# Chunk attention and two gated products on one core: opening, loads around the bursts, banks and sums in another order

## The chip, the cores and the metric

The kernel runs on one core of a Trainium2 chip. The metric is the device time of one execution in microseconds (us), the median of several runs; the profile and the trace are of one further execution.

## What is computed

The reference, cut to what matters (q, k and v are 8 x 8 x 576 x 64, float32):

```python
q_c, k_c, v_c = (t.reshape(8, 8, 9, 64, 64) for t in (q, k, v))   # chunks of 64
scores = scale * q_c @ k_c.transpose(0, 1, 2, 4, 3)
attn = softmax(scores)                                            # per row, 1e-9 in the divisor
x = (attn @ v_c) -> tokens x 512                                  # 4608 x 512
x = (x @ w_a) * (x @ w_b) @ w_out                                 # inner width 1536
out = ((x @ w1) * (x @ w2)) @ w3 @ w_out2                         # inner width 1024
```

## The kernel before

**Tiles and stages.** The 4608 tokens are 9 blocks of 512. The first gated product goes through its inner width in 12 slices f of 128, the second in 8. All large products are kept accurate by splitting each operand into a high part and a low part (fp32r) and doing three TensorE (PE) products for each one wanted. For a block and a slice, the first products x·w_a and x·w_b are `pa` and `pb` (L901), their gated product is split into `gh` and `gl` (L287 on ScalarE, L288), and the second product with `wo` is summed over f in four PSUM banks (`acc`, L944).

- *Opening.* Attention of block 0 is done unit by unit (a unit is one pair of heads of one block; `U[0]` to `U[3]`): load q and k (`load1`), load v (`load2`), `turn` (transposes `t`, copies `qT`, `kT`), `scores` (`s`), `soft1` (maximum `mx`, exponent `e`), `soft2` (sum `sm`, its reciprocal, a multiplication of `e`), `flip` (`f`, `pT`), `apply` (`x`), `put`. Beside it the weights w_a, w_b and w_out are converted into their two parts by jobs of the class Pump: three VectorE (DVE) operations L209, L212 and L220 with a ScalarE one between, then a ScalarE cast and a low part (L725 on VectorE for w_a and w_b, on GpSimd for w_out). `pump.load` issues a job's load, `begun` its first part, `run` its second part and the low part of the job before, `flush` the low part alone.
- *Plain steps.* Blocks 0 and 1, slice by slice, with `pa` and `pb` (`plain_step`). The first slices of block 0 come while weights are converted.
- *Burst.* The gated products of a pair's second block are kept, and its second products are done all in a row: 12 slices of 12 `acc` products (`burst`). Such a slice needs its `wo`, 512 KB, loaded into one of four places.
- *Pass over a pair.* Blocks 2 and 3, 4 and 5, 6 and 7 go as pairs by Strassen's scheme: seven products P1 to P7 (L914) per slice on three banks, whose sums ScalarE copies (L1001) and VectorE adds (L1005); VectorE's L1034 makes the gated product (`strassen_step`). In the first pass VectorE also makes the sums of weights `su` that the scheme needs, and the attention of blocks 4 and 5. A burst stands between two passes.
- *Block 8 alone.* After the last burst come plain steps of block 8, and between them w3·w_out2 is made on the chip: parts of w3 are turned on PE (`w3p`, L1174) into `w3t`, and multiplied (`wf`, L1185), all on PSUM bank D. w_out2 and w3 come by small loads `o_0` to `o_7` and `w3_0` to `w3_15` (`load_small`, L1142) into four places; a part `o` is split into its two parts by `one` in `o2_pieces`, called from the burst.
- *Second gated product.* The same with w1, w2 and the fused weight.

**What sets the order.** Every engine works through its own instructions in the order of the code, and a DMA is issued by an engine's queue in the order of its instructions; a queue that waits holds all behind it. Nearly all loads are issued on SP's queue. The loads of attention units are put on a list (`ask`), and taken off it by `settle` (all that a unit needs) and by `tick(loads=n)`, which precedes each group of PE products; the number of `tick` in a `first` group is `state["pace"]`. VectorE work that can lie anywhere is cut into pieces, and a `Track` hands them out at the `point()` calls of a step; it keeps an estimate of how far PE and VectorE have come (class Engines) and holds a piece back where VectorE is ahead of that by `backlog`, or where a piece with PE work (`needs`) would come before `self.ready`.

## Time and profile before

| | |
|---|---|
| median of 3 runs | 1621.13 us (1620.41 to 1628.59) |
| profiled execution | 1621.47 us |
| its span in the trace | 1619.7 us |
| PE busy, idle | 1546.9 us, 72.8 us |
| opening, to the end of U[3] and the first slices | 0 to 113.2 us |
| plain steps | 113.2 to 262.2 us |
| first burst, first pass over a pair | 262.2 to 305.4, 305.4 to 478.3 us |
| second burst, second pass | 478.3 to 517.6, 517.6 to 675.1 us |
| third burst, third pass | 675.1 to 711.4, 711.4 to 864.8 us |
| last burst, block 8 with w3·w_out2 | 864.8 to 907.2, 907.2 to 1062 us |
| second gated product | 1062 to 1619.7 us |

The stages are cut where PE's first product of the next one starts. PE is the engine that is busy nearly always, so what can be read as lost is PE's idle time and the time in which its products run longer than elsewhere. In the trace's own times 1.8 us of the profiled execution lie outside the span.

### The profile page before, as it was taken

Reading aid. Unit: us, or ns where it says so; the run is one execution under the profiler, and the core shown is the slowest. Engines: PE = TensorE matmul, PEld = TensorE weight load, DVE = VectorE, ACT = ScalarE, POOL = GpSimd, SP = SyncE. Lnnn points to the kernel's source line nnn. Section 1 sums busy time; section 2 is a strip of 40 time slices with the busy share of each in tenths; the row PEclk is TensorE's granted clock in tenths of the full one; section 3 lists DMA queues with packets and bytes.
Section 4 is the critical chain, followed back from the end, with each engine's and each line's share of the span. In section 5 each row is a group of like instructions: output and inputs, shape, how many; then the busy total and the mean of one; then the engine's idle time right before and its main releaser. Section 6 shows DMA issues by size and latency. Waiting matters only on the chain.

```text
span 1619.7 us, 24157 instructions
## 1 busy us (share of the span) xinstructions
PE 1546.9 (96%) x8968; PEld 1254.5 (77%) x8968; DVE 856.1 (53%) x1384; ACT 539.9 (33%) x997; POOL 491.0 (30%) x502
## 2 busy tenths in 40 slices
PE   5689999998999999999999899999999999999998
PEld 4568787776777787888787777888878878878887
DVE  5767564776757555576775235545532442442431
ACT  4444444332334222433334223333421421421322
POOL 0323324322234211433235212223522422422422
PEclk9889999998999999999999999999999999999999
...
GB/s 245 216 240 266 255 152 187 262 218 225 241 100 216 200 226 218 130 211 342 334 292 171 286 318 325 300 275 256 115 226 221 74 223 222 74 217 209 68 289 155
DMA packets 277013, 356.31 MB, mean 220 GB/s; under 512 B 174240, under 2 KB 194720, under 8 KB 276896
## 3 DMA queue, kind: packets, MB, share of 16 engines
...
HBM read 268.70 MB, written 85.98 MB: 219 GB/s over the span
## 4 chain that ended last, share of the span: by engine, by line
PE 80%; DVE 7%; issue 4%; DMA 3%; ACT 3%; SPq 2%; POOL 1%; DVEq 0%; POOLq 0%; ACTq 0%
PE P L914 41%; PE acc L944 22%; PE pa L901 4%; PE pb L901 4%; PE wf L1185 3%; PE pa0L L901 2%; DMA wo<-dwo 1%; PE x L442 1%; SPq L181 1%; PE s L390 1%; PE pb0L L901 1%; DVE c L1005 1%; PE t L519 1%; DMA qk<-in_k_dram 1%; ACT xP L287 1%
## 5 line engine op out<-in xcount | busy, mean ns | idle before, releaser
L914 PE MATMUL P<-xP,w 128*128 128x512 f32 (+1 forms) x3066 | 698.3, 381 | 13.7 <-DVE c L1005 8.5
L914 PEld LDWEIGHTS P<-xP,w 128*128 128x128 f32 x3066 | 553.8, 189 | 129.8 <-DVE c L1005 12.6
L1005 DVE TENSOR_TENSOR c<-P,c 128x512 f32<-128x512 f32 (+1 forms) x228 | 150.5, 661 | 322.2 <-PE P L914 321.7
L1001 ACT COPY c<-P 128x512 f32<-128x512 f32 (+1 forms) x228 | 128.6, 564 | 226.4 <-PE P L914 226.1
L1036 POOL TENSOR_TENSOR G<-c,c 128x512 f32<-128x512 f32 x68 | 89.3, 1313 | 319.6 <-DVE c L1005 319.5
L287 ACT CAST gh<-c 128x512 fp32r<-128x512 f32 x68 | 42.2, 621 | 316.6 <-DVE c L1034 316.6
L288 POOL TENSOR_TENSOR gl<-c,gh 128x512 fp32r<-128x512 f32 x68 | 90.7, 1333 | 177.6 <-ACT gh L287 177.6
L944 PE MATMUL acc<-gh,wo 128*128 128x512 f32 x384 | 138.3, 397 | 0.0
L944 PE MATMUL acc<-wo,gh 128*128 128x512 f32 x320 | 111.0, 390 | 0.5 <-ACT gh L287 0.5
L1034 DVE TENSOR_TENSOR c<-P,c 128x512 f32<-128x512 f32 x68 | 46.9, 689 | 120.9 <-PE P L914 120.9
L901 PE MATMUL pa<-xq,w 128*128 128x512 f32 x276 | 76.5, 431 | 9.9 <-DVE w L725 9.9
L944 PEld LDWEIGHTS acc<-gh,wo 128*128 128x128 f32 x384 | 72.4, 188 | 15.5
L288 DVE TENSOR_TENSOR xP<-xP,xP 128x512 fp32r<-128x512 f32 (+1 forms) x56 | 65.4, 1209 | 22.9 <-ACT xP L287 22.9
L944 PE MATMUL acc<-gl,wo 128*128 128x512 f32 x192 | 75.0, 391 | 0.0
L901 PEld LDWEIGHTS pa<-xq,w 128*128 128x128 f32 x276 | 56.3, 209 | 23.7 <-DVE w L725 10.4
L944 PEld LDWEIGHTS acc<-wo,gh 128*128 128x128 f32 x320 | 60.1, 188 | 13.0 <-ACT gh L287 1.0
L901 PE MATMUL pb<-xq,w 128*128 128x512 f32 x276 | 68.5, 397 | 0.0
L954 ACT COPY ev<-acc 128x512 f32<-128x512 f32 x72 | 42.4, 588 | 72.9 <-PE acc L944 67.9
L944 PE MATMUL acc<-wo,gl 128*128 128x512 f32 x160 | 62.5, 390 | 0.8 <-POOL gl L288 0.8
L190 POOL DMA_DIRECT2D dw<-w x58 | 31.8, 551 | 89.8 <-DVE w L288 85.8
L901 PEld LDWEIGHTS pb<-xq,w 128*128 128x128 f32 x276 | 50.5, 188 | 10.4
L408 ACT ACTIVATE e<-e 128x512 f32<-128x512 f32 x36 | 22.8, 633 | 107.0 <-DVE e L402 103.2
...
## 6 DMA issues: line engine op xcount, KB each, us to landing
...
wo<-dwo SPq DMA_DIRECT2D x128, 512.0 KB, 4.5
...
```

What stands on the lines that cost most here:

```text
L190: queue.dma_start(to, src)
L287: nc.scalar.copy(dst_h, src)
L288: eng_l.tensor_tensor(dst_l, src, dst_h, op=ALU.subtract)
L901: nc.tensor.matmul(ps, w[m][:, kk // 2, wp, kk % 2], xq[kk // 2][:, kk % 2, xp], start=(begins and n == 0), stop=(ends and n == len(terms) ...
L914: nc.tensor.matmul(ps, w[:, wp, kt], x[:, kt, xp], start=(begins and n == 0), stop=(n == 5), skip_group_check=True,)
L944: nc.tensor.matmul(acc[m], a, b, start=(f == 0 and (wp, gp) == SEQ[0]), stop=(f == NF[ph] - 1 and (wp, gp) == SEQ[-1]),)
L954: nc.scalar.copy(t, acc[m])
L1001: nc.scalar.copy(t, src)
L1005: nc.vector.tensor_tensor(o, a, b, op=ALU.add)
L1034: nc.vector.tensor_tensor(g, last, c11, op=ALU.mult)
L1036: nc.gpsimd.tensor_tensor(g_place(ph, nm.split("_")[0], f, gplaces), c22, c12, op=ALU.mult)
L1185: nc.tensor.matmul(ps, t[:, gp, jj], wo2[jj // 2][:, jj % 2, wp], start=(jj == 0 and (wp, gp) == SEQ[0]), stop=(jj == NF[1] - 1 and (wp, g ...
```

## The change

It has five groups of edits.

1. *Opening.* q and k of U[3] are asked for earlier, v of U[0] and U[1] later (behind the transposes and the exponent of U[0]; both are issued on ScalarE's queue). Job 1 is begun after `soft2` of U[3] rather than amid the attention of U[0] to U[3]; jobs further on follow its low parts sooner, with `pump.ahead` 0 or 1 for a while; `flush` and `scores` move.
2. *Loads around bursts.* The pace of unit loads at the end of the plain steps goes from 5 to 9. What was spread over the first burst (sums of weights and weights, six loads) is issued ahead of it. Ahead of the last burst three conversion loads are issued at once; the first four w3 loads become pieces of it.
3. *Small loads.* `load_small` issues on ScalarE's queue instead of SP's (24 loads).
4. *Banks.* `w3p` and `wf` take turns on banks B and D.
5. *Order of sums and pieces.* In a Strassen step the sums with P3 and P7 follow each other, and the point for pieces comes after both. `Track` waits 0.9 us rather than 0.3 after a piece with PE work, and the backlog is 2.0 in two places (2.5, and none, before). Conversions in the first slices are handed out over 2 points rather than 5.

```diff
@@ -95,7 +95,7 @@
             if e and needs and cost < 1:
                 self.ready = e.pe + 1.5
             elif e and cost > 0.5:
-                done = e.computed(cost) + 0.3
+                done = e.computed(cost) + (0.9 if needs else 0.3)
                 if needs is not None:
...
@@ -1016,9 +1016,9 @@
         freed(1)
         point()
         add(c12, take("P3"), c12)
-        point()
         add(c22, take("P7"), c22)
         freed(2)
+        point()
         pend.part()
         pend.part()
         point()
...
     wo2, w3f, w3t = [], deque(), {}
-    small = {"n": 0}
+    small = {"n": 0, "bank": 0}
+
+    def either(name):
+        small["bank"] += 1
+        return bank("BD"[small["bank"] % 2], name)
 
     def load_small(src, name):
         small["n"] += 1
         t = pool.tile([P, NT], F32, tag=["qk0", "qk1", "ep0", "ep1"][small["n"] % 4], name=name)
-        nc.sync.dma_start(t, src)
+        nc.scalar.dma_start(t, src)
         return t
 
     def o2_pieces():
@@ -1169,7 +1173,7 @@
         w = w3f.popleft()
         if c == 0:
             w3t[i] = pool.tile([P, 2, NF[1], P], F32R, tag=f"G{i % 2}", name=f"w3t_{i}")
-        ps = bank("D", f"w3p_{i}_{c}")
+        ps = either(f"w3p_{i}_{c}")
         for m in range(4):
             nc.tensor.transpose(ps[:, m * P : (m + 1) * P], w[:, m * P : (m + 1) * P], ident)
         t = w3t[i]
@@ -1179,7 +1183,7 @@
 
     def fuse(i):
         t = w3t.pop(i)
...
@@ -1259,11 +1263,11 @@
                 load()
             settle(asks["all"])
 
-        asked(U[0].load1, U[1].load1, U[0].load2, U[1].load2)
+        asked(U[0].load1, U[1].load1)
         pump.load()
-        asked(U[2].load1)
+        asked(U[2].load1, U[3].load1, U[2].load2)
         pump.load()
-        asked(U[3].load1, U[2].load2, U[3].load2)
+        asked(U[3].load2)
         pump.load()
 
         plain = {0: {}, 1: {}}
@@ -1285,11 +1289,13 @@
             pump.begin(n)
 
         U[0].turn()
+        asked(U[0].load2)
         U[0].scores()
         pump.load()
         U[1].turn()
         U[0].soft1()
         begun(1)
+        asked(U[1].load2)
         U[1].scores()
         U[2].turn()
         U[0].soft2()
@@ -1297,7 +1303,6 @@
         U[1].soft1()
         pump.load()
         asked(U[4].load1)
-        begun(2)
         U[1].soft2()
         U[0].apply()
         U[0].put()
@@ -1307,7 +1312,6 @@
         U[2].soft1()
         pump.run()
         pump.load()
-        pump.run()
         U[1].apply()
         U[3].scores()
         U[3].soft1()
@@ -1315,6 +1319,9 @@
         U[1].put()
         U[2].flip()
         U[3].soft2()
+        pump.flush()
+        begun(2)
+        pump.run()
         pump.load()
         pump.load()
         pump.load()
@@ -1322,7 +1329,6 @@
         asked(U[5].load1)
         U[2].apply()
         U[2].put()
-        pump.flush()
         U[3].flip()
         xq = [quadrants[0, 0], quadrants[0, 1]]
         banks = [bank("AC"[m], f"p{m}0") for m in range(2)]
@@ -1333,7 +1339,8 @@
 
         features(0, [0, 1])
         U[3].apply()
-        pump.begin(pump.done + 1)
+        pump.flush()
+        begun(pump.done + 1)
         U[3].put()
         features(0, [2])
         U[4].turn()
@@ -1345,14 +1352,16 @@
         nc.scalar.copy(sa, banks[0])
...
         asked(U[4].load2)
+        U[4].scores()
         pump.run()
-        U[4].scores()
+        pump.ahead = 1
+        pump.run()
         U[4].soft1()
+        pump.flush()
         nc.vector.tensor_tensor(sa, banks[1], sa, op=ALU.mult)
         state["pending"] = Second(0, 0, 0, wouts[0], g_parts(sa, "0_0_0", nc.gpsimd), sums[0])
-        pump.run()
+        pump.ahead = 2
         pump.load()
-        pump.flush()
         U[5].load2()
         tick(loads=4)
         units = unit_list(1)
@@ -1363,7 +1372,8 @@
         at = None
         for n, (T, f) in list(enumerate(order))[1:]:
             if T == 0:
-                conv = Track([conv_piece()] * (4 if f == 1 else 3), 5 if f + 1 < AHEAD else 8, engines)
+                ahead = f + 1 < AHEAD
+                conv = Track([conv_piece()] * (4 if f == 1 else 3), 2 if ahead else 8, engines)
                 if f + 1 == NF[0]:
                     conv = None
             if T == 1 and f == 0:
@@ -1382,7 +1392,7 @@
             if n + 3 == len(order):
                 at.finish()
                 next_units(2)
-                state["pace"] = 5
+                state["pace"] = 9
             if n + 1 == len(order):
                 state["ready"] = ready(0, 1, NF[0] - 2, plain[0])
...
@@ -1423,7 +1433,7 @@
                     if k + 2 < n:
                         su[k + 2] = summed(ph, order[k + 2], k + 2)
                         su[k + 2].load()
-                    extra = Track(su[k + 1].pieces() if k + 1 < n else [], 5, engines)
+                    extra = Track(su[k + 1].pieces() if k + 1 < n else [], 5, engines, 2.0)
                 if whole_new:
                     if READY <= f + 2 < n:
                         su[f + 2] = Sums(ph, f + 2, dict(tag=f"Y{f % 2}"))
@@ -1528,20 +1538,17 @@
                 pieces = pieces + o2_pieces()
                 pump.cap = len(pump.jobs)
                 pump.homes(["xo1", "xo2"], ["G2"])
-                pieces += [(0.1, False, lambda: pump.load())] * 3
+                for _ in range(3):
+                    pump.load()
+                pieces += [(0.1, False, lambda n_=n_: load_w3(n_)) for n_ in range(4)]
             elif not begins:
                 x, pieces = strassen_pieces(x32, f"{ph}{sb}", sb == NSB)
             if ph == 0 and sb == 1:
-                begins_with = []
                 for n_ in range(2):
                     first_sums[n_] = summed(ph, orders[ph, sb][n_], n_)
-                    begins_with.append((0.1, False, first_sums[n_].load))
-                for n_, i in ((0, 0), (0, 3), (1, 0), (1, 3)):
-                    begins_with.append(
-                        (0.1, False, lambda f=orders[ph, sb][n_], i=i: load_part(ph, f, i))
-                    )
-                for n_, p in enumerate(begins_with):
-                    pieces.insert(4 + 3 * n_, p)
+                    first_sums[n_].load()
+                    for i in (0, 3):
+                        load_part(ph, orders[ph, sb][n_], i)
                 pieces = pieces + first_sums[0].pieces()
             steps, at, conv = NF[ph], [], []
             if ph == 0 and not lone:
@@ -1557,14 +1564,12 @@
                     conv = later_conv(3 * NF[1])
                     work = merged((0, 1, work), (0, 1, conv))
                     n_pts = PTS * steps
-                at.append(Track(work, n_pts - 1 if sb + 1 < NSB else n_pts - 3, engines, 2.5))
+                at.append(Track(work, n_pts - 1 if sb + 1 < NSB else n_pts - 3, engines, 2.0))
             if not begins:
                 done = (ph, sb - 1) if sb else (ph, 0)
                 burst(ph, j + 1, orders[done], places, pieces, [] if conv else at, state.pop("ready", None))
             if lone:
                 got = []
-                for n_ in range(4):
-                    load_w3(n_)
                 at.append(Track(between(got), 5 * steps - 15, engines))
                 xs = {}
 
```

Where it moves instructions, in three places.

**VectorE in the opening**, behind the sum `sa_0_1` of slice 1 (cv is a conversion, `sm` and `e` the softmax of unit U[4], w_2_0 the low part that slice 2's `pa` takes). Before:

```order
L1065 TENSOR_TENSOR sa_0_1_753<-pb_0_1_761,sa_0_1_753 128x512
L209 TENSOR_SCALAR cv_xo_556<-cv_xo_556 128x512
L212 SCALAR_TENSOR_TENSOR cv_xo_397<-cv_xo_556 128x512
L220 SCALAR_TENSOR_TENSOR cv_xo_397<-cv_xo_556,cv_xo_397 128x512
L413 TENSOR_REDUCE sm_0_808<-e_0_709 128x8
L414 TENSOR_SCALAR sm_0_808<-sm_0_808 128x8
L415 RECIPROCAL sm_0_808<-sm_0_808 128x8
L416 TENSOR_TENSOR e_0_709<-e_0_709,sm_0_808 128x512
L209 TENSOR_SCALAR cv_Y_266<-cv_Y_266 128x512
L212 SCALAR_TENSOR_TENSOR cv_Y_267<-cv_Y_266 128x512
L220 SCALAR_TENSOR_TENSOR cv_xo_397<-cv_xo_556,cv_xo_397 128x512
L725 TENSOR_TENSOR w_2_0_792<-cv_xo_397,w_2_0_792 128x2x256
```

After:

```order
L1065 TENSOR_TENSOR sa_0_1_750<-pb_0_1_769,sa_0_1_750 128x512
L209 TENSOR_SCALAR cv_Y_260<-cv_Y_260 128x512
L212 SCALAR_TENSOR_TENSOR cv_Y_261<-cv_Y_260 128x512
L220 SCALAR_TENSOR_TENSOR cv_xo_397<-cv_xo_557,cv_xo_397 128x512
L725 TENSOR_TENSOR w_2_0_766<-cv_xo_397,w_2_0_766 128x2x256
```

A conversion triple and the four softmax rows no longer stand ahead of the low part w_2_0; they stand behind w_3_0 now, or earlier.

**SP's queue around the first burst** (qk and v are loads of attention units, su and w those of the first pass, wo those of the burst). Before, from the burst's first load of a `wo` on:

```order
L181 DMA qk_1_2808<-in_q_dram 32x8x32 x4
L782 DMA wo_7_2991<-dwo_7_171 128x1024
L181 DMA qk_1_2808<-in_q_dram 32x8x32 x2
L819 DMA su_11_3005<-d_0_11_155 128x1024
L819 DMA su_10_3012<-d_0_10_154 128x1024
L181 DMA qk_1_2808<-in_q_dram 32x8x32 x2
L181 DMA qk_1_2808<-in_k_dram 32x8x32 x2
L797 DMA w_11_0_3039<-dw_11_0_108 128x1024
L181 DMA qk_1_2808<-in_k_dram 32x8x32 x2
L782 DMA wo_6_3054<-dwo_6_170 128x1024
L181 DMA qk_1_2808<-in_k_dram 32x8x32 x2
L799 DMA w_11_3_3068<-dw_11_1_109 128x512
```

After:

```order
L181 DMA v_1_2809<-in_v_dram 64x2x64 x4
L819 DMA su_11_2957<-d_0_11_155 128x1024
L797 DMA w_11_0_2959<-dw_11_0_108 128x1024
L799 DMA w_11_3_2961<-dw_11_1_109 128x512
L819 DMA su_10_2963<-d_0_10_154 128x1024
L797 DMA w_10_0_2965<-dw_10_0_104 128x1024
L799 DMA w_10_3_2967<-dw_10_1_105 128x512
L782 DMA wo_7_3025<-dwo_7_171 128x1024
L782 DMA wo_6_3074<-dwo_6_170 128x1024
L782 DMA wo_5_3101<-dwo_5_169 128x1024
L782 DMA wo_4_3126<-dwo_4_168 128x1024
```

The loads of the unit and the six for the pass stand ahead of wo_7 now, and the four `wo` loads follow each other.

**VectorE in the first pass**, slice 7 (the two L1005 rows are the sums with P3 and with P7; `sm`, `e` and `pT` are the softmax of a unit). Before:

```order
L1005 TENSOR_TENSOR c_7_3955<-P_7_3882,c_7_3955 128x512
L413 TENSOR_REDUCE sm_3_4000<-e_3_3979 128x8
L414 TENSOR_SCALAR sm_3_4000<-sm_3_4000 128x8
L415 RECIPROCAL sm_3_4000<-sm_3_4000 128x8
L416 TENSOR_TENSOR e_3_3979<-e_3_3979,sm_3_4000 128x512
L1005 TENSOR_TENSOR c_7_3889<-P_7_3918,c_7_3889 128x512
L422 STREAM_TRANSPOSE pT_3_4024<-e_3_3979 128x512
```

After:

```order
L1005 TENSOR_TENSOR c_7_3991<-P_7_3912,c_7_3991 128x512
L1005 TENSOR_TENSOR c_7_3922<-P_7_3953,c_7_3922 128x512
L413 TENSOR_REDUCE sm_3_4021<-e_3_3947 128x8
L414 TENSOR_SCALAR sm_3_4021<-sm_3_4021 128x8
L415 RECIPROCAL sm_3_4021<-sm_3_4021 128x8
L416 TENSOR_TENSOR e_3_3947<-e_3_3947,sm_3_4021 128x512
L422 STREAM_TRANSPOSE pT_3_4033<-e_3_3947 128x512
```

The sum with P7 stands right behind the sum with P3, and the four softmax rows behind both.

No engine has more or fewer instructions to compute with; ScalarE issues 24 DMAs more and SP 24 fewer.

## Rows read from the trace of the kernel before

**Rows 1.** The page, part 1: busy time, share of the span, instructions.
```profile
PE 1546.9 (96%) x8968; PEld 1254.5 (77%) x8968; DVE 856.1 (53%) x1384; ACT 539.9 (33%) x997; POOL 491.0 (30%) x502
```

**Rows 2.** Busy time by stage (windows): engines, granted clock, DMA share, GB/s.
```profile
0.00:113.20 113.20, 77.99 (x784) 61.19 (x784) 76.40 (x147) 51.38 (x99) 26.93 (x37) 0.86 0.83 232
262.19:305.42 43.23, 39.10 (x188) 30.68 (x189) 35.24 (x47) 19.34 (x35) 20.56 (x19) 0.96 0.84 246
305.42:478.28 172.86, 163.67 (x1115) 128.96 (x1114) 115.34 (x214) 49.91 (x95) 45.27 (x49) 0.97 0.69 209
517.56:675.06 157.50, 156.72 (x1114) 125.66 (x1114) 81.15 (x152) 38.48 (x72) 32.29 (x27) 1.00 0.74 204
675.06:711.40 36.34, 36.33 (x160) 29.77 (x160) 29.21 (x27) 18.55 (x33) 21.50 (x18) 1.00 0.49 162
864.84:907.19 42.35, 38.33 (x160) 30.62 (x159) 17.31 (x15) 17.31 (x31) 19.20 (x18) 0.96 0.59 204
```

**Rows 3.** TensorE's waits, 0 to 122 us: total us, times, longest us.
```profile
PE pa L901 <- DVE w L725: 9.9, 2, 5.5
PE t L519 <- DMA qk<-in_q_dram: 6.1, 1, 6.1
```

**Rows 4.** Timeline of ScalarE and its DMA queue, 0 to 10 us: start, us.
```profile
3.58 4.72 ACTq L181 DMA_DIRECT2D v<-in_v_dram  x4
8.33 1.28 ACT L520 ACT_TABLE_LOAD   x1 [8.33 <-DMA v<-in_v_dram]
```

**Rows 5.** Timeline of TensorE, 46 to 80 us, plain products.
```profile
46.49 5.25 PE L901 MATMUL pa<-xq,w 128*128 128x512 f32 x12 [5.45 <-DVE w L725]
51.58 2.88 PE L901 MATMUL pb<-xq,w 128*128 128x512 f32 x12
...
62.49 5.49 PE L901 MATMUL pa<-xq,w 128*128 128x512 f32 x12 [4.41 <-DVE w L725]
```

**Rows 6.** Timeline of VectorE, 54 to 63 us.
```profile
54.57 0.69 DVE L1065 TENSOR_TENSOR sa<-pb,sa 128x512 f32<-128x512 f32 x1 [5.70 <-PE pb L901]
...
57.97 0.67 DVE L413 TENSOR_REDUCE sm<-e 128x8 f32<-128x512 f32 x1
...
61.75 0.69 DVE L725 TENSOR_TENSOR w<-cv_xo,w 128x512 fp32r<-128x512 f32 x1
```

**Rows 7.** Line L220, 0 to 122 us: ns min/median/max.
```profile
L220 DVE SCALAR_TENSOR_TENSOR cv_xo<-cv_xo,cv_xo x8: 682/686/1796, 44.1 to 98.9; 128x512 int32<-128x512 int32 x8
```

**Rows 8.** TensorE's waits in the first burst, 262 to 306 us.
```profile
PE acc L944 <- DMA wo<-dwo: 4.1, 3, 2.5
```

**Rows 9.** Timeline of SP's DMA queue, 264 to 277 us.
```profile
265.27 0.36 SPq L782 DMA_DIRECT2D wo<-dwo  x1
...
275.93 0.34 SPq L782 DMA_DIRECT2D wo<-dwo  x1
```

**Rows 10.** TensorE's waits in the first pass over a pair, 306 to 478 us.
```profile
PE P L914 <- DVE c L1005: 5.4, 5, 1.8
PE P L914 <- DVE c L1034: 3.0, 1, 3.0
```

**Rows 11.** Busy time in part of that pass.
```profile
360.00:400.00 40.00, 35.13 (x219) 27.24 (x218) 26.29 (x50) 9.75 (x18) 7.60 (x8) 0.87 0.70 202
```

**Rows 12.** Timeline of VectorE, 385 to 394 us.
```profile
392.01 0.71 DVE L379 STREAM_TRANSPOSE kT<-qk 128x512 f32<-128x512 f32 x1 [3.74 <-DMA v<-in_v_dram]
```

**Rows 13.** TensorE's waits in the last burst, 860 to 905 us.
```profile
PE acc L944 <- DMA wo<-dwo: 4.0, 2, 2.3
```

**Rows 14.** Timeline of SP's DMA queue, 876 to 884 us.
```profile
880.47 2.02 SPq L1142 DMA_DIRECT2D o<-do  x2
882.55 0.42 SPq L782 DMA_DIRECT2D wo<-dwo  x1
```

**Rows 15.** TensorE's waits in the steps of block 8, 905 to 1060 us.
```profile
PE w3p L1174 <- DVE w3t L288: 3.5, 6, 1.7
PE wf L1185 <- DVE w3t L288: 1.3, 3, 0.7
```

2 lines of the change are left out of this document (1 added, 1 removed).

## Prediction

> **What bounds the kernel now.** I read the table of engines first. TensorE (PE) is busy for 1546.9 us of a span of 1619.7 [rows 1], so 72.8 us of idle time are all that a better order can win there, besides products that run slow. VectorE, at 53%, bounds no long stage; where it counts, it is late with one result.
>
> Then the stages, beside the same kind of stage without trouble [rows 2]. In the opening PE is busy for 77.99 of 113.20 us, at a granted clock of 0.86 of full speed. The first burst took 43.23 us, and the last 42.35; the third did the same products in 36.34, at 1.00. The first pass over a pair took 172.86 us and the second 157.50, where VectorE had 115.34 and 81.15 us to do. So the losses lie at the opening, two bursts and the first pass. These are where the change works, and in each I looked for what ended the waits.
>
> The profiled execution took 1621.47 us, 0.34 over the median of the runs; the sum is made against 1621.5, and the 1.8 us outside the span are taken as they are.
>
> **Opening.** PE waits 9.9 us in two places for VectorE's low part of a weight, and 6.1 for the first q and k [rows 3]. The two waits are ahead of the `pa` of slices 1 and 2. In the rows of PE, the `pa` behind them took 5.25 and 5.49 us, where the `pb` that followed took 2.88 for the same 12 products [rows 5]: the clock had fallen while PE waited. So each wait is paid about twice. On VectorE, the sum of slice 1 ended at 55.26 us, and the low part came at 61.75, after a conversion, four softmax rows from 57.97 on, and another conversion [rows 6]. The change takes the softmax and one of the two conversions out of this row, that is, the 3.78 us from 57.97 to 61.75, of a wait of 4.41 [rows 5, 6]. In slice 1 the low part moves ahead of the maxima and differences of U[4]. For both waits I take 8 of 9.9 us. Of the slow `pa`, 5.25 + 5.49 − 2 × 2.88 = 5.0 us over the fast price, I take 3.
>
> At the start, ScalarE issues the four DMAs of v for 4.72 us from 3.58 us on, and its table load follows them at 8.33 [rows 4]. With v behind, ScalarE's first copy can come sooner, and q and k share the DMA engines with less. I take 2.5 of at most 4.72.
>
> Against this, L220, the last step of a conversion, took 682 ns at best and 1796 at worst among eight [rows 7]. Which rows stand beside a GpSimd row changes; two slow ones more would be 2.2 us, and I take off 1.5. The Trainium skill, "SBUF — State Buffer", section "SBUF: two separate sides", says that a VectorE operation with two inputs in SBUF and a GpSimd operation that reads SBUF lock one shared pair of ports, and that the later one fully blocks. The rows agree as far as a spread goes, and show no lock.
>
> Sum: 8 + 3 + 2.5 − 1.5 = **12 us less**. Bounds: nothing of the clock or the start, and half the waits, less 2.2, is 3; all that was named and nothing taken off would be 19.6, but the stage's other work is unchanged, and I stop at 16.
>
> **First burst.** PE waits three times for a `wo`, 4.1 us [rows 8]. SP issues wo_7 at 265.27 us and wo_6 at 275.93 [rows 9], 10.7 us apart, and loads of q and k, sums of weights and weights stand between. The change puts all of these ahead of wo_7, and then the `wo` one behind the other. Beside the clean burst 43.23 − 36.34 = 6.9 us are lost [rows 2]; the 2.8 that are no wait fit the clock of 0.96, since 4% of 43.23 is 1.7. I take **5 us less**, between 1 (the six loads, put in front, delay wo_7 in their turn) and 6.5.
>
> **First pass.** 172.86 − 157.50 = 15.4 us are what it costs over the next pass [rows 2]; its extra products and attention turns on PE are some of it. PE waits 5.4 us in five places for VectorE's sums L1005, and once 3.0 for L1034 [rows 10]. In the slice shown above, softmax of four rows stands between the sums with P3 and P7, and P7's sum frees what PE needs next; now it stands behind both. That mends about 4 of 5.4. The wait for L1034 is at 392: VectorE waited 3.74 us for a transposition whose operand was late [rows 12], and the sum was queued behind it. The loads of units now come together and ahead of weights, and I take 2 of 3.0. A stretch around these waits ran at 0.87 [rows 11]: 13% of its 40 us are 5.2, and I take 2 back. Sum: **8 us less**, between 2 (VectorE's 115.34 us stay, and the wait moves to another piece) and 14 (5.4 + 3.0 + 5.2). The later backlog of 2.0 and the wait of 0.9 in `Track` only reorder the same pieces; I cost them at nothing, covered by the 57 us in which VectorE is idle here. If that cover is gone, softmax comes too late and its products wait, at about the 4 us that I credit to the order.
>
> **Last burst.** Two waits for a `wo`, 4.0 us [rows 13], at a clock of 0.96 that costs 1.7 [rows 2]. On SP a pair of small loads took 2.02 us, because the first of them waited for its place, and a `wo` was issued only behind them, at 882.55 [rows 14]. ScalarE issues them now, so SP is free. But ScalarE then waits for the place instead, and behind it stand the casts of `gh` that the burst's products take. I take **2 us less**, between 4 more (the same 4.0 once again on ScalarE) and 5.7 less. The Trainium skill, "DMA: Bandwidth & Descriptors", section "Issuing engines are not separate DMA queues", says that issuing from several engines only saves the sequencer's time of issuing, usually little beside the transfer. By that this term would be nothing. The row speaks for a queue that waits, which is more than issue time.
>
> **Block 8.** `w3p` waits 3.5 us in six places for VectorE to have emptied the one bank D, and `wf` 1.3 in three [rows 15]. With two banks, PE turns the next part while the last is emptied. I take **3 us less**, between 0 (VectorE is late in any case) and 4.8.
>
> **The rest**: pace 9 instead of 5, conversions over 2 points instead of 5, loads pulled ahead. No instruction is added, and PE's 148 us in the plain steps hide them; nothing, with at most 2 us either way.
>
> 12 + 5 + 8 + 2 + 3 = 30 us, and 1621.5 − 30 = **1591.5 us**. With all upper bounds it would be 1574, with all lower ones 1619.5.
>
> **Rivals.**
>
> *The transfers pace the opening.* The stage has a DMA share of 0.83, and no stage above shows more than 0.84 [rows 2]. If 0.84 is the ceiling, 113.20 × 0.83 / 0.84 = 111.9 us are the least for the bytes, and 1.3 us the gain. Against it: part of the bytes are for later slices and can wait. 1621.5 − 19.3 = 1602.
>
> *VectorE stays the bound in the first pass.* For it: 115.34 us in 172.86 [rows 2], in rows that come in clusters. Then 2 instead of 8: 1597.5.
>
> *The small loads gain nothing on ScalarE*, and its casts wait as SP did: 4 more instead of 2 less in the last burst, 1597.5 as well.
>
> *Slower: ScalarE is held by its 24 new issues.* Four issues of v took 4.72 us, 1.18 each [rows 4]. If the casts and copies behind each are what PE waits for, and each issue also waits as long again for its place, 24 × 2.36 = 57 us are added, against 25 that opening, first burst and first pass win: 1653. It decides from (25 + 8) / 24 = 1.4 us of each issue in PE's sight. Against it: ScalarE is busy only 33% of the time [rows 1], and small loads took about 1 us each on SP [rows 14].
>
> *The order wins nothing*: waits move to the next piece, all terms at their lower bounds or near, and less than 8 us are seen: 1613 to 1629.
>
> **How the numbers follow.** Forecast 0.50; transfers 0.13; VectorE 0.11; small loads 0.08; no gain 0.10; slower 0.08. 0.5%, or 8 us, is about what a measurement of this kernel can tell from no change. The forecast and the first three rivals are faster, 0.82; no gain is "same", 0.10; ScalarE's is slower, 0.08. The forecast's own range is 1580 to 1603, its larger terms at their bounds one at a time. The 8-in-10 range goes on to the rivals at 1597.5 and 1602 with the other terms low, so to 1612, and below to 1578, where the opening and the first pass give most of their upper bounds; no gain and slower are left out, 0.18.
>
> **What would show it.** Opening: no wait of `pa` for the low part longer than 1 us, and both `pa` near 2.9 us; the stage near 101 us. First burst near 38 us with no wait for `wo` above 1 us. First pass near 165, with L1005 waits under 2 us in all. Last burst near 40 us, and no idle time of `acc` put down to `gh`. Block 8: `w3p` waits near none. Wrong it would be if PE's idle time in the opening goes to the first turn or softmax instead, if a `wo` is late behind the six loads, or if ScalarE's rows show DMA issues of over 1.4 us with PE waiting behind.

## The result, and the profile after

The changed kernel takes 1606.26 us (median of 4 runs, 1600.32 to 1609.44) for 1622.00 of the kernel before (1620.41 to 1628.59); the ratio is 0.9895, with a 95% interval of 0.9864 to 0.9926. It is faster by 1.05%, some 16 us, where 30 were forecast. The profiled execution took 1609.44 us, the slowest of the four, 12.0 under that of before.

The table of engines, PE's row: its work is the same within 1.3 us of [rows 1], and its idle time fell from 72.8 to 62.0 us.

```profile
PE 1545.6 (96%) x8968; PEld 1255.6 (78%) x8968; DVE 859.0 (53%) x1384; ACT 538.4 (33%) x997; POOL 492.6 (31%) x502
```

Busy time by stage, with the columns of [rows 2]; the stages are the opening, the first burst, the first pass, the second burst and the last burst:

```profile
0.00:108.88 108.88, 78.49 (x784) 62.31 (x784) 78.01 (x147) 51.04 (x99) 26.98 (x37) 0.88 0.84 241
258.95:304.98 46.03, 40.16 (x189) 31.87 (x190) 34.00 (x47) 19.36 (x35) 20.57 (x19) 0.89 0.62 205
304.98:474.02 169.04, 160.85 (x1115) 125.76 (x1114) 117.33 (x214) 49.23 (x95) 45.44 (x49) 1.00 0.71 214
474.02:517.16 43.14, 40.01 (x193) 31.76 (x191) 33.96 (x38) 19.06 (x34) 21.82 (x18) 0.92 0.59 162
...
865.73:902.65 36.92, 36.65 (x161) 29.68 (x159) 16.05 (x15) 17.51 (x31) 19.10 (x18) 1.00 0.75 255
```

Against [rows 2] the opening went from 113.20 to 108.88 us (the plain steps behind it gave 1.1 of these 4.3 back), the first pass from 172.86 to 169.04 and the last burst from 42.35 to 36.92. But the first burst became longer, 46.03 for 43.23, at a clock of 0.89. The second, at 43.14 for 39.28 before, lost 3.9 us where nothing had been forecast.

Cut by the rows of `acc`, where a burst's products begin and end (up to 0.2 us beside the windows above), the two profiled executions divide like this, in us:

| stage | before | after | change | forecast |
|---|---|---|---|---|
| opening and plain steps | 262.19 | 258.95 | −3.2 | −12 |
| first burst | 43.23 | 46.03 | +2.8 | −5 |
| first pass | 172.70 | 169.04 | −3.7 | −8 |
| second burst | 39.28 | 43.14 | +3.9 | 0 |
| second pass, third burst, third pass | 347.28 | 348.57 | +1.3 | 0 |
| last burst | 42.51 | 36.92 | −5.6 | −2 |
| block 8, up to the next burst | 251.91 | 244.41 | −7.5 | −3 |
| the rest of the span | 460.60 | 460.54 | −0.1 | 0 |

**Opening.** PE's waits, in the columns of [rows 3]: the two waits for the low part fell from 9.9 to 6.3 us, not to 2, and two waits for v are new.

```profile
PE pa L901 <- DVE w L725: 6.3, 2, 3.9
...
PE x L442 <- DMA v<-in_v_dram: 3.1, 2, 1.7
```

The two `pa` behind the waits, on PE's timeline (start, us, rows as in [rows 5]). The first is now fast, the second still slow:

```profile
47.33 3.06 PE L901 MATMUL pa<-xq,w 128*128 128x512 f32 x12 [2.39 <-DVE w L725]
...
61.77 4.48 PE L901 MATMUL pa<-xq,w 128*128 128x512 f32 x12 [3.90 <-DVE w L725]
```

VectorE's timeline ahead of the second:

```profile
52.14 1.52 DVE L209 TENSOR_SCALAR cv_xo<-cv_xo 128x512 int32<-128x512 uint32 x1
...
54.31 0.69 DVE L220 SCALAR_TENSOR_TENSOR cv_xo<-cv_xo,cv_xo 128x512 int32<-128x512 int32 x1
54.91 0.42 DVE L209 TENSOR_SCALAR cv_xo<-cv_xo 128x512 int32<-128x512 uint32 x1
...
55.97 1.79 DVE L220 SCALAR_TENSOR_TENSOR cv_xo<-cv_xo,cv_xo 128x512 int32<-128x512 int32 x1
57.69 0.68 DVE L1065 TENSOR_TENSOR sa<-pb,sa 128x512 f32<-128x512 f32 x1
...
59.34 1.76 DVE L220 SCALAR_TENSOR_TENSOR cv_xo<-cv_xo,cv_xo 128x512 int32<-128x512 int32 x1
61.03 0.68 DVE L725 TENSOR_TENSOR w<-cv_xo,w 128x512 fp32r<-128x512 f32 x1
```

GpSimd's timeline over the same time, its operations on tensors:

```profile
51.90 1.48 POOL L288 TENSOR_TENSOR gl<-sa,gh 128x512 fp32r<-128x512 f32 x1 [4.36 <-ACT gh L287]
...
55.73 1.48 POOL L751 TENSOR_TENSOR wo<-cv_xo,wo 128x512 fp32r<-128x512 f32 x1 [1.84 <-ACT wo L754]
59.09 1.47 POOL L288 TENSOR_TENSOR gl<-sa,gh 128x512 fp32r<-128x512 f32 x1 [1.88 <-ACT gh L287]
```

The row that the prediction relied on is there: behind the sum `sa` (57.69) come one conversion and the low part (61.03), with no softmax. But the sum itself begins at 57.69 us, 54.57 before [rows 6], since two conversions stand ahead of it now, where before it was one; the conversion that left the place behind the sum came back ahead of it. And three of the operations took 1.52, 1.79 and 1.76 us, for 0.42 (L209) and 0.69 (L220) beside them. Each begins some 0.24 us after a GpSimd operation of 1.48 and ends 0.3 to 0.6 after that one ends. Such rows are not new, though. The kernel before had one behind the same sum, 0.24 us behind the start of a GpSimd operation (56.01 to 57.50 us), and one of 1.76 at 44.07:

```profile
56.25 1.80 DVE L220 SCALAR_TENSOR_TENSOR cv_xo<-cv_xo,cv_xo 128x512 int32<-128x512 int32 x1
```

Over the first 122 us, seven conversion rows before and nine after took 1.3 us or more; beyond the usual duration of their line that is 7.4 us before and 9.1 after.

The first burst begins at 258.95 us here. Over all profiles of the study it begins at 261.4 to 263.1 in the four without the opening's edits, and at 255.6 to 259.0 in the seven that have all of them: some 5 us on average, of which this pair of executions shows 3.2.

**First burst.** PE's waits in it:

```profile
PE acc L944 <- DMA wo<-dwo: 3.4, 1, 3.4
PE s L390 <- DVE kT L379: 2.5, 1, 2.5
```

SP's queue, then VectorE's turn of a unit's q:

```profile
262.04 19.66 SPq L782 DMA_DIRECT2D wo<-dwo  x6
290.60 0.86 SPq L181 DMA_DIRECT2D qk<-in_q_dram  x2
291.56 0.44 SPq L782 DMA_DIRECT2D wo<-dwo  x1
```

```profile
289.28 0.70 DVE L378 STREAM_TRANSPOSE qT<-qk 128x512 f32<-128x512 f32 x1
```

SP issued nothing between 281.70 and 290.60 us. What it then issued is q of the next unit, into the place that VectorE's turn at 289.28 frees; the `wo` stands behind, is issued at 291.56, and PE, out of work for 3.4 us, goes on at 297.22. So the pile of loads that spread over the burst before [rows 9] is gone, and the same queue is held by a wait, which ended when VectorE's second turn, of k, was done at 290.58.

**First pass.** In the columns of [rows 10]:

```profile
PE P L914 <- DVE c L1034: 5.2, 5, 1.8
PE P L914 <- DVE c L1005: 2.1, 2, 1.9
```

Five waits for L1005 became five for L1034: the softmax that left the place between two sums stands ahead of the next operation that PE waits for. One such place on VectorE, with both sums in the first row (x2), the softmax from the second row on and L1034 in the last:

```profile
325.58 1.28 DVE L1005 TENSOR_TENSOR c<-P,c 128x512 f32<-128x512 f32 x2
326.78 0.67 DVE L413 TENSOR_REDUCE sm<-e 128x8 f32<-128x512 f32 x1
...
330.94 0.69 DVE L1034 TENSOR_TENSOR c<-P,c 128x512 f32<-128x512 f32 x1
```

All in all the waits shrank little: PE was idle for 9.2 us of the pass before and for 8.2 now. The other 2.7 us are products that no longer run slow. Behind the longest wait before, 30 products took 9.97 us; behind the wait in the same place now they take 7.11:

```profile
393.35 9.97 PE L914 MATMUL P<-xP,w 128*128 128x512 f32 x30 [3.03 <-DVE c L1034]
```

```profile
389.29 7.11 PE L914 MATMUL P<-xP,w 128*128 128x512 f32 x30 [1.75 <-DVE c L1034]
```

VectorE's late turns are not gone. It waited once, 3.74 us, for an operand of a turn before [rows 12]; now it waits for k three times, 6.9 us in all, at the longest here:

```profile
411.49 0.71 DVE L379 STREAM_TRANSPOSE kT<-qk 128x512 f32<-128x512 f32 x1 [3.95 <-DMA qk<-in_k_dram]
```

### The profile page after: what moved, and what is told of

The parts are those of the page before. It is cut to its first block, busy times and chain, and to the rows that moved or that the text cites. A ratio compares the mean times of both kernels' runs of the same rounds, so it can differ in the third digit from the quotient of the medians.

```text
span 1607.6 us, 24155 instructions
## 1 busy us (share of the span) xinstructions
PE 1545.6 (96%) x8968; PEld 1255.6 (78%) x8968; DVE 859.0 (53%) x1384; ACT 538.4 (33%) x997; POOL 492.6 (31%) x502
## 4 chain that ended last, share of the span: by engine, by line
PE 81%; DVE 7%; DMA 4%; issue 3%; ACT 2%; SPq 1%; POOL 1%; DVEq 0%; ACTq 0%; POOLq 0%
PE P L914 39%; PE acc L944 23%; PE pa L901 4%; PE pb L901 4%; PE wf L1189 3%; PE pb0L L901 2%; PE pa0L L901 2%; DVE xP L288 2%; DMA wo<-dwo 2%; PE x L442 1%; SPq L181 1%; PE s L390 1%; DMA qk<-in_k_dram 1%; DMA v<-in_v_dram 1%; ACT xP L287 1%
## 5 line engine op out<-in xcount | busy, mean ns | idle before, releaser
L1005 DVE TENSOR_TENSOR c<-P,c 128x512 f32<-128x512 f32 (+1 forms) x228 | 150.0, 661 | 320.4 <-PE P L914 319.7
L1034 DVE TENSOR_TENSOR c<-P,c 128x512 f32<-128x512 f32 x68 | 47.0, 691 | 124.7 <-PE P L914 124.6
L901 PE MATMUL pa<-xq,w 128*128 128x512 f32 x276 | 72.4, 414 | 6.3 <-DVE w L725 6.3
```

The costliest lines, as they stand in the source:

```text
L901: nc.tensor.matmul(ps, w[m][:, kk // 2, wp, kk % 2], xq[kk // 2][:, kk % 2, xp], start=(begins and n == 0), stop=(ends and n == len(terms) ...
L1005: nc.vector.tensor_tensor(o, a, b, op=ALU.add)
L1034: nc.vector.tensor_tensor(g, last, c11, op=ALU.mult)
```

## The experiments

The edits of the change are named by the number of their group in the section on the change. "Kernel C" is the changed kernel with one number put back, the first experiment. Each was timed beside the kernel before, on the same chip; the chips differ (experiments 1 to 4, 5 to 8, 9 to 11, and 12), and the kernel before took 1622.07, 1623.44, 1619.01 and 1623.18 us on them. So a difference of up to 4 us between the medians of two such groups says nothing.

**1. The backlog of 2.0 (kernel C).**

```diff
-                at.append(Track(work, n_pts - 1 if sb + 1 < NSB else n_pts - 3, engines, 2.0))
+                at.append(Track(work, n_pts - 1 if sb + 1 < NSB else n_pts - 3, engines, 2.5))
```

> The changed kernel with one number put back: the backlog of the Track that hands out attention pieces in bursts and passes is 2.5 again, not 2.0. In the changed kernel the first burst took 46.03 us and the second 43.14 (before 43.23 and 39.28). Theory A: with 2.0 the turn of a unit (VectorE L378, L379) is handed out later; it frees the place for the next unit's q, for which SP waits (from 281.70 to 290.60 us), and a wo load stands behind. Then with 2.5 the turn comes before the sums of weights, the first two bursts together fall from 89.2 us to 78 to 82, the wait of acc for a wo falls from 3.4 and 1.4 us to under 1, and the time falls by 6 to 10 us against the changed kernel. Theory B: the unit loads and six pass loads issued ahead are what delays wo, by their transfer; then the bursts stay at 46 and 43 us within 1.5 and the time stays. The first pass should stay at 169 us by A; by a third reading, in which 2.0 is what won 3.7 us there, it goes back to 172.

It took 1596.68 us, ratio 0.9828 (0.9802 to 0.9853), which lies clear of the changed kernel's interval: 9.6 us by the medians. The first burst took 43.39 us and the second 40.64, 84.0 in sum: a fall of 5.1, where 7 to 11 were expected. The opening of this execution was 2.8 shorter too, with the same code, so the rows place 5 of the 9.6 us and no more. SP's queue, then VectorE's turn:

```profile
259.28 14.18 SPq L782 DMA_DIRECT2D wo<-dwo  x4
280.73 0.83 SPq L181 DMA_DIRECT2D qk<-in_q_dram  x2
281.66 0.39 SPq L782 DMA_DIRECT2D wo<-dwo  x1
```

```profile
279.42 0.70 DVE L378 STREAM_TRANSPOSE qT<-qk 128x512 f32<-128x512 f32 x1
```

The turn comes 23.2 us after the burst's start (279.42 − 256.20) and not 30.3 (289.28 − 258.95), and SP goes on right behind it. The waits:

```profile
PE s L390 <- DVE kT L379: 3.6, 1, 3.6
PE acc L944 <- DMA wo<-dwo: 1.3, 1, 1.3
```

The wait for `wo` fell to 1.3 us, not under 1 as A has it, and PE's scores now wait longer for the turn itself. The first pass stayed at 169.24: the backlog of 2.0 won nothing there.

**2. Only the edits around block 8 (groups 3 and 4, and the loads of group 2 at the last burst), on the kernel before.**

```diff
-        nc.sync.dma_start(t, src)
+        nc.scalar.dma_start(t, src)
-        ps = bank("D", f"w3p_{i}_{c}")
+        ps = either(f"w3p_{i}_{c}")
...
-                pieces += [(0.1, False, lambda: pump.load())] * 3
+                for _ in range(3):
+                    pump.load()
+                pieces += [(0.1, False, lambda n_=n_: load_w3(n_)) for n_ in range(4)]
```

> The kernel before with only the edits around the last burst and block 8: small loads issued on ScalarE, banks B and D in turn, three conversion loads at once ahead of the burst, the first four w3 loads as pieces of it. In the changed kernel the last burst won 5.6 us and block 8 up to the second gated product's first burst 7.5. Theory A: these 13 us come from these edits alone; then the time is 13 us below before (12 to 14), with the last burst near 37 us, no w3p or wf wait, and every other stage as before within 1 us. Rival: part of it comes from the earlier stages (loads that ran ahead, another order of pieces in the third pass); then under 9 us are won here.

1611.00 us, ratio 0.9908 (0.9879 to 0.9937). The last burst and the steps of block 8 in its profile:

```profile
867.48:903.84 36.36, 36.35 (x160) 29.78 (x159) 16.84 (x15) 17.49 (x31) 19.09 (x18) 1.00 0.75 257
903.84:1050.00 146.16, 146.16 (x673) 120.41 (x672) 75.23 (x124) 49.09 (x89) 31.44 (x42) 1.00 0.90 324
```

PE is busy throughout at full clock. With the part behind the second window, block 8 up to the next burst took 244.41 us, as in the changed kernel: 6.1 + 7.5 us against before, and A holds for these two stages. It does not hold for the others, which were to stay within 1 us: the first burst of this execution took 45.48 us with no edit near it, 2.3 more than before, and the third pass took 1.2 more. The medians differ by 11.1 us, for the 12 to 14 of A. A burst of this kind varies by some 2 us between executions.

**3. Only the opening (group 1), on the kernel before.** The diff is the part of the change's from `asked(U[0].load1` to `tick(loads=4)`, and the two points for conversions.

> The kernel before with only the edits of the opening (loads, begun, flush, run, scores, two points for conversions). In the changed kernel the first burst began 3.2 us earlier. Theory A: the opening wins 1.4 us at the start (table load) and 3 to 6 us at the low parts, and gives 4.7 back because v of the second unit lands late, so 3 us (2 to 5) are left, and the time is 3 us below before. Rival: the opening by itself wins the 12 us that were forecast and another edit costs 9 of them (the Track's 0.9, which also holds pieces of the plain steps); then the first burst starts near 250 us and the time is about 12 us below.

1616.12 us, ratio 0.9973 (0.9946 to 1.0000). The first burst began at 257.64 us for 262.19: 4.6 us, within what A gives, and nothing near 12.

**4. Only the order of sums and the numbers of Track (group 5, but for the two points), on the kernel before.**

```diff
-                done = e.computed(cost) + 0.3
+                done = e.computed(cost) + (0.9 if needs else 0.3)
...
-        point()
         add(c22, take("P7"), c22)
         freed(2)
+        point()
...
-                    extra = Track(su[k + 1].pieces() if k + 1 < n else [], 5, engines)
+                    extra = Track(su[k + 1].pieces() if k + 1 < n else [], 5, engines, 2.0)
...
-                at.append(Track(work, n_pts - 1 if sb + 1 < NSB else n_pts - 3, engines, 2.5))
+                at.append(Track(work, n_pts - 1 if sb + 1 < NSB else n_pts - 3, engines, 2.0))
```

> The kernel before with only the order of sums (P3 and P7 adjacent) and the three numbers of Track (0.9; backlog 2.0 for the sums of weights and for the attention pieces). Theory A: the first pass wins 3 to 4 us, its waits for L1005 fall from 5.4 to about 2 us, the waits for L1034 rise to about 5; the backlog of 2.0 makes the first two bursts 3 to 4 us longer each, as in the changed kernel, so in sum the time is 2 to 5 us above before. Rival: the longer bursts in the changed kernel come from the loads issued ahead of them; then the bursts stay at 43.2 and 39.3 us and the time is 3 to 4 us below before.

1620.73 us, ratio 0.9977 (0.9955 to 0.9999). The second burst, where no load was moved, went from 39.28 to 43.32 us, as in the changed kernel: with the first experiment this shows the backlog as the cause there. The first burst took 45.72 and the first pass 168.12. The two sides nearly cancel, but A's sum, 2 to 5 us above before, is wrong: the pass won 4.6, and the last burst and block 8 were 3.9 shorter than in the one profile of before, with no edit near them. PE's waits in the pass moved as A says, from L1005 (1.0 us left) to L1034 (4.4).

Alone, the edits of experiments 2, 3 and 4 win 0.92, 0.27 and 0.23%, 1.42 in sum, where the whole change wins 1.05; the intervals are too wide to tell these apart. More than half of the gain is around block 8.

**5. Kernel C without attention in the bursts.**

```diff
-    burst(ph, j + 1, orders[done], places, pieces, [] if conv else at, state.pop("ready", None))
+    burst(ph, j + 1, orders[done], places, pieces, [], state.pop("ready", None))
```

> The changed kernel with the backlog of 2.5, and no attention piece handed out during a burst (all of it in the passes). With 2.5 the first two bursts took 43.39 and 40.64 us, with 5.3 us of waits for kT (3.6 and 1.7) and 1.3 for a wo. Theory A: attention in a burst costs twice, by PE's scores that stand behind a turn that is late on VectorE, and by SP's queue, where q of the next unit waits for the turn ahead of a wo. Then without it both bursts go to 36.4 to 38 us, 9 us less, and the first pass takes up to 6 us more, since VectorE has about 8 us more to do there; in sum 3 to 9 us below the kernel with 2.5 (1596.7). Rival: VectorE's lateness in the first pass takes all of it (its pieces come in clusters between sums), the pass takes 9 to 12 more, and the time is the same or higher.

1614.47 us, 18 more than C. First burst, first pass, second burst, second pass:

```profile
257.25:295.31 38.06, 36.13 (x156) 29.23 (x157) 31.00 (x34) 18.73 (x34) 20.56 (x19) 1.00 0.70 247
295.31:473.11 177.80, 162.83 (x1147) 128.39 (x1146) 122.21 (x227) 50.35 (x96) 45.39 (x49) 0.97 0.69 206
473.11:509.46 36.35, 36.35 (x160) 29.76 (x159) 28.12 (x25) 18.43 (x33) 21.82 (x18) 1.00 0.63 179
509.46:678.25 168.79, 160.81 (x1146) 128.61 (x1145) 89.13 (x165) 39.11 (x74) 32.62 (x27) 0.97 0.70 194
```

The bursts came out as A says (38.06 and 36.35), so attention pieces are what they lose by, but for 1.9 us in the first, in which PE waits for a part `gl` from GpSimd. But the passes took 8.6 and 12.0 more than C's 169.24 and 156.80, and the rival decides. Part of it is work that did not fit and is done at the end of the pass, where PE waits once in each of the two for a unit's softmax, which VectorE does from 451.53 to 458.14 us in the first (the view finds no releaser for the wait, hence `issue`):

```profile
457.32 0.44 PE L442 MATMUL x<-pT,v 64*64 64x64 f32 x2 [5.75 <-issue]
```

**6. Kernel C with the opening's loads as before.**

```diff
-        asked(U[0].load1, U[1].load1)
+        asked(U[0].load1, U[1].load1, U[0].load2, U[1].load2)
         pump.load()
-        asked(U[2].load1, U[3].load1, U[2].load2)
+        asked(U[2].load1)
         pump.load()
-        asked(U[3].load2)
+        asked(U[3].load1, U[2].load2, U[3].load2)
...
-        asked(U[0].load2)
...
-        asked(U[1].load2)
```

> The changed kernel with the backlog of 2.5, and the loads of the opening as in the kernel before: v of U[0] and U[1] ahead of the table load, q and k of U[3] and v later on SP; the other edits of the opening stay. In the changed kernel the first scores came 1.4 us earlier (9.37 for 10.75), but PE waited 3.1 us for v of U[1] and the first product x with w_a began 3.3 us later (35.15 for 31.87). Theory A: the late v is what eats the opening's gain; then with v early that product begins at 30 to 32.5 us and the first burst 2 to 4 us earlier (252.5 to 254.5 for 256.2), the time 2 to 4 us lower. Rival: the conversions on VectorE bound the stage (the low part that pa of slice 1 takes comes when it comes); then pa waits the longer for the low part and the first burst begins at 256 to 258, no gain.

1596.95 us, ratio 0.9829 (0.9798 to 0.9859): no other time than C. PE's timeline, the first product with w_a:

```profile
30.04 2.13 PE L901 MATMUL p<-xq,w 128*128 128x512 f32 x6
```

In this one profile the product came at 30.04 us and the burst at 252.47, as A has it. But experiment 9, with the same opening, had them at 31.94 and 256.26, and C itself at 33.17 and 256.20. So the late v costs that product 1 to 3 us, and the times do not show that it costs the kernel anything. The burst begins at 252.47, 256.26 and 255.96 us in the three kernels with v early, 254.9 on average, and at 257.0 on average in the seven with v late: up to 2 us may be due to it, or none, and the rival stands.

**7. Kernel C with the loads around the first burst as before** (pace 5, six loads spread over the burst: the first of group 2).

> The changed kernel with the backlog of 2.5, and the loads around the first burst as in the kernel before: pace 5, and the six loads for the pass spread over the burst. Theory A: putting them ahead wins what was forecast in part: with them spread the three waits for a wo of 4 to 6 us are back, and the first burst takes 2 to 4 us more than 43.4, the first pass the same, the time 2 to 4 us more than 1596.7. Rival: the burst is bound by attention pieces (kT, and q's place) whatever the order of loads; then the burst stays at 43 to 44 us, the time within 1.5 us.

1600.90 us, ratio 0.9855 (0.9826 to 0.9885), on the same chip as experiment 6. The first burst took 44.02 us, for 43.39 and 41.73 in C and experiment 6. PE's waits in it:

```profile
PE acc L944 <- DMA wo<-dwo: 6.1, 4, 2.2
```

The waits for a `wo` are back, as A has it, and no wait for kT is among PE's waits, where C has 3.6 us: to put the loads ahead exchanged one wait for another. By the times the direction is A's, but the intervals overlap and the burst differs by less than two profiles of one code do. All profiles with a backlog of 2.5 and attention in the bursts say a little more: the first burst took 41.7 to 43.7 us in the six with the loads ahead and 43.2 to 45.9 in the five with them spread (four of these without the other edits too), some 2 us on average, for the 5 that were forecast.

**8. Only the two banks (group 4), on the kernel before.**

```diff
-        ps = bank("D", f"w3p_{i}_{c}")
+        ps = either(f"w3p_{i}_{c}")
...
-        ps = bank("D", f"wf_{i}")
+        ps = either(f"wf_{i}")
```

> The kernel before with only the two banks for w3p and wf. With all edits around block 8 that stage went from 251.9 to 244.4 us (7.5 less), where the waits of w3p and wf were 5.3 us. Theory A: the bank was the wait: 5 to 7.5 us less in that stage by the banks alone, the last burst as before (40 to 42.5 us). Rival: the small loads and the weights behind them on SP are the cause of part of it; then the banks alone win under 4 us there, and w3p waits for its load.

1613.51 us, ratio 0.9935 (0.9914 to 0.9955), 10 us less. In its profile, which is of the slowest run (1620.00), block 8 took 249.97 us. PE's waits there:

```profile
PE w3p L1178 <- DMA w<-dw: 3.6, 1, 3.6
```

All waits for VectorE [rows 15] are gone, so the bank was what they waited for. One late small load stands in their place, and in this execution the stage is only 1.9 us shorter than before, which is the rival's case, while the median of all runs fits A. How much of the 7.5 the banks win alone depends on that load.

**9. Experiment 6 with the scores later in bursts.**

```diff
-                done = e.computed(cost) + (0.9 if needs else 0.3)
+                done = e.computed(cost) + (0.9 if needs else self.margin)
...
                 for a in at:
+                    a.margin = 4.0
                     a.point()
+                    a.margin = 0.3
```

> The kernel with backlog 2.5 and the opening's loads as before, and one number more: during a burst a piece with PE work is held back until 4.0 us, not 0.3, after the estimated end of the piece before it. The scores of the first unit then stand four groups of acc products later on PE in both bursts; the order of loads is the same. In that kernel without it the first two bursts took 41.73 and 39.03 us, of which PE waited for kT 1.7 us in the second. Theory A: the scores wait on PE for a turn that VectorE does later than the estimate, and the clock falls behind the wait; with the scores later no wait for kT above 0.5 us is left, the second burst takes 36.4 to 37.5 us, the first 38 to 40.5, and the time is 2 to 5 us lower. Rival: softmax and the second turn follow the scores, so the next unit comes later, its q frees its place later on SP, and a wo is late instead: bursts as before within 1 us, or the passes take back what they win.

1597.80 us, ratio 0.9868 (0.9847 to 0.9888): no faster than C. Its waits in the first burst:

```profile
PE acc L944 <- DMA wo<-dwo: 4.0, 2, 2.8
...
PE s L390 <- DVE kT L379: 0.8, 1, 0.8
```

The wait for kT fell to 0.8 in the first burst and to nothing in the second, which took 37.87 us, 1.2 less than in experiment 6 but over A's 36.4 to 37.5. In the first a `wo` is late instead, as the rival has it, and it took 43.56; nor is the time lower, so the rival decides.

**10. Kernel C with the small loads on SP** (group 3 undone).

```diff
-        nc.scalar.dma_start(t, src)
+        nc.sync.dma_start(t, src)
```

> The changed kernel with the backlog of 2.5, and the small loads issued on SP's queue again (the conversion loads at once and the w3 loads as pieces stay, the two banks too). With them on ScalarE the last burst took 36.4 us, as the undisturbed third, and block 8 up to the second gated product's first burst 244.4. Theory A: a small load that waits for its place on SP holds the wo behind it; then the last burst goes back to 39 to 42 us with a wait for wo of 2 to 4 us, and block 8 to 246 to 250 as a small load behind weights comes late; the time 4 to 9 us more than 1596.7. Rival: issuing from another engine saves only the time of issuing; then both stages stay within 1 us, and the last burst won by the order of the loads alone.

1599.40 us, ratio 0.9882 (0.9867 to 0.9897). The last burst took 38.85 us, for 36.37 in C, with these waits:

```profile
PE acc L944 <- DMA wo<-dwo: 1.9, 2, 1.4
```

Block 8 took 244.44, as with ScalarE. So the queue is worth 2.5 us in the last burst by this pair, and nothing behind it: A holds for the burst alone, the rival for block 8. It is one profile, though: of the nine kernels with all edits for this burst eight took 36.4 to 37.7 us for it and experiment 12 took 40.37, so 1.2 to 2.5 us is as near as the record comes. In the four kernels without the edits around block 8's loads the burst took 40.0 to 42.5 us, so the other 1.2 to 3.7 come from the three conversion loads at once and the w3 loads as pieces, edits that were costed at nothing; they were not tried alone.

**11. Kernel C with the old order of sums.**

```diff
         add(c12, take("P3"), c12)
+        point()
         add(c22, take("P7"), c22)
         freed(2)
-        point()
```

> The changed kernel with the backlog of 2.5, and the point for pieces between the sums with P3 and P7 again. The first pass took 167.99 to 169.24 us in the kernels with all of group 5 (backlog 2.0 or 2.5) and 171.3 to 173.0 in those without. Theory A: it is the place of softmax between the two sums; then the pass goes back to 171 to 173 with waits for L1005 of 4 to 7 us, and the time is 2 to 4 us more than 1596.7. Rival: the numbers of Track (0.9, and the backlog of the sums of weights) did it; then the pass stays at 169 within 1 us.

1595.88 us, ratio 0.9860 (0.9840 to 0.9880). The first pass, and PE's waits in it:

```profile
299.20:463.64 164.44, 159.80 (x1114) 126.49 (x1113) 114.33 (x214) 49.44 (x95) 45.02 (x49) 0.99 0.72 220
```

```profile
PE P L914 <- DVE e L402: 2.3, 2, 1.6
PE P L914 <- DVE c L1005: 2.3, 2, 2.1
```

Theory A falls, and more than that: with the point between the sums the pass is 4.8 us shorter than C's, and no wait for L1034 is left; experiment 12, with the same order, has 165.88, and the seven others with the new order and attention in the bursts 167.5 to 169.3. What won the first pass is then in the numbers of Track, the wait of 0.9 or the backlog of the sums of weights: the loads changed nothing there (168.12 without them in experiment 4, 168.05 in 7), nor did the other backlog. The two were not tried apart. PE was idle for 9.2 to 11.7 us of the pass in the four kernels without these numbers and for 4.6 to 8.2 in the nine that have them and attention in the bursts, at a clock of 0.97 to 1.00 and of 0.98 to 1.00: over all profiles the gain is in the waits, and the pair of the result section, where it was mostly the clock, is the exception. The median is C's all the same. The two profiles differ by 5.8 us, but that of C is of its slowest run, 4.7 above its median, and the chips differ, so whether the old order wins time stays open.

**12. Joined: experiments 6 and 11, and v of U[0] and U[1] issued by GpSimd.**

```diff
-            return nc.sync, *[nc.scalar if early else nc.sync] * 2
+            return nc.sync, nc.scalar if early else nc.sync, nc.gpsimd if early else nc.sync
```

> The changed kernel with the backlog of 2.5, the old order of the sums with P3 and P7, the opening's loads as before, and v of U[0] and U[1] issued by GpSimd, which has nothing else to do then, so that ScalarE's table load need not wait. Theory A (opening bound by single late operands): first scores near 9.4 us, no wait of x for v, first product x with w_a at 28 to 30 us, first burst from 250 to 253.5 us; with a first pass of 164 to 165 us the time is 1588 to 1593. Rival (the first 60 us are paced by the transfers: their DMA share was 0.92 to 0.97 there in nearly all kernels so far): an earlier v only makes q, k or the weights later, the low parts come when they come, the first burst begins at 254 to 257 us, and the time is 1593 to 1597, no better than the best so far (1595.9).

1595.72 us, ratio 0.9826 (0.9810 to 0.9842): no better than C. PE's timeline, the first scores and the first product with w_a:

```profile
9.68 1.14 PE L390 MATMUL s<-kT,qT 64*64 64x64 f32 x32 [0.68 <-ACT kT L520]
...
31.76 2.91 PE L901 MATMUL p<-xq,w 128*128 128x512 f32 x6
```

The first scores came early and no `x` waited for v, yet the first burst began at 255.96. The last burst took 40.37 us, with a wait for a `wo` of 2.1, though all the edits made for it are in. That `wo` was issued at 873.23 us, 2.7 behind the one before it like its neighbours, and landed only at 880.64, 7.4 us later; in C the `wo` of this burst landed 3.3 to 4.6 us behind their issue. So it was the transfer that was late here and not the queue; what slowed it isn't settled. The first 60 us of the span:

```profile
0.00:60.00 60.00, 38.97 (x418) 31.56 (x419) 40.62 (x81) 26.97 (x50) 13.93 (x22) 0.91 0.94 242
```

In the first 60 us the DMA share is 0.94; it is 0.91 to 0.97 in twelve of the fourteen kernels (0.93 in the kernel before), 0.88 in experiment 5 and 0.84 in the changed one. The rival holds as far as an earlier v moves nothing. That the transfers pace these 60 us is not shown, since no run took bytes away; that VectorE's conversions do, the rival of experiment 6, fits as well, since `pa` waited 6.3 us for the low part in this run too.

## Why the prediction was right in sign and wrong in size

- *The opening, 12 forecast, 3.2 measured in the pair and some 5 over all profiles.* The step that failed is "The change takes the softmax and one of the two conversions out of this row". The row was read from the sum `sa` on, and what now stands ahead of the sum was not read: two conversions. The 1.5 us set aside for operations slowed beside GpSimd were about right: 9.1 us here for 7.4 before are 1.7 more, although three in this one place cost 3.3 (1.52 + 1.79 + 1.76 − 0.42 − 2 × 0.69), since two of 1.76 and 1.80 lay ahead of these low parts before. The rule of the Trainium skill that was set beside that term ("SBUF — State Buffer", section "SBUF: two separate sides", one pair of ports, the later one blocked) fits the rows here: each of the three ends only after the GpSimd operation that began first. One of them, L209, has a single input; the same section of the Trainium skill has such an operation take the pair only in a two-port mode, and no row shows the mode. Of 8 us of waits 3.6 were won, of the 5.0 of slow `pa` 2.2 behind the first wait and 1.0 behind the second (3.06 and 4.48 for 5.25 and 5.49), and 3.1 us of waits for v were added, a price of the late v that the sum did not have. The table load did come early (3.47 us for 8.33), and the first scores 1.4 us sooner, for 2.5 forecast. The rival of transfers took 0.84 as the ceiling of the DMA share; in the same trace the first 60 us ran at 0.93 and the steps of block 8 at 0.88, so its ceiling was wrong. Its sum, 1.3 us of gain, came nearer to the stage than the forecast, and whether its reading is the right one stays open.
- *The first burst, 5 less forecast, 2.8 more measured.* The mechanism, unit loads that pile up between two `wo`, was right, and it was removed. The failed step is "and then the `wo` one behind the other": SP came to the next unit's q sooner, and held a `wo` behind that load while it waited for a turn. The backlog of 2.0, costed at nothing "covered by the 57 us in which VectorE is idle here", made that turn 7 us later than 2.5 does. It costs in the second burst too (43.1 and 43.3 us in the two kernels with 2.0, 37.9 to 40.6 in those with 2.5 and attention there), and by experiment 1 the two bursts pay some 5 us for it. The prediction named the way, softmax too late when the cover is gone, at the wrong place: bursts, where VectorE is busy for 35 of 43 us [rows 2], not the pass.
- *The first pass, 8 forecast, 3.7 measured.* "That mends about 4 of 5.4" is wrong: the order of sums only moved the waits to L1034 (8.4 us for both lines before, 7.3 now), and with it undone the pass is some 3 us shorter (164.4 and 165.9 us in experiments 11 and 12, 168.4 on average in the seven with the new order). In this pair the gain is by the clock, as forecast and a little more (2.7 us in PE's products, for 2, with the stage's granted clock at 1.00 for 0.97): no wait is longer than 1.9 us now, for 3.0, and no group of products behind one runs slow. The late turn, 2 of 3.0 forecast, was not mended. What else was costed at nothing, the numbers of `Track`, is what shortens the waits over all profiles (experiment 11).
- *The last burst, 2 forecast, 5.6 measured.* The mechanism was right. The queue is worth 1.2 to 2.5 (experiment 10). The term was mis-sized because the three loads and the order of w3, 1.2 to 3.7 us, were left out. The rule of the Trainium skill that issuing from several engines only saves issue time ("DMA: Bandwidth & Descriptors", section "Issuing engines are not separate DMA queues") would have given 0; what was won is the wait of a queue, which is no issue time, so the rule and the run don't contradict each other, but going by it would have missed this. ScalarE's 24 issues cost nothing that a row shows, and the slower rival is out.
- *Block 8, 3 forecast, 7.5 measured.* Right in kind: no wait of `w3p` or `wf` is left; they were 4.8 us for VectorE [rows 15] and 0.5 for a load. The rest is PE's own rows, 147.35 us for 149.52 for the same 678 products. The upper bound of 4.8 was drawn from the waits alone.

So the sum came within its range by luck as much as by its terms, through errors of both signs: 21 us too much at the beginning, 8 too little at the end, and 5 lost in places that had no term. The forecast's own range ended at 1603, below the 1606.26 measured; the wider one, to 1612, holds it because it was drawn on for two rivals.
